# Issuing a kernel's weight stores from ScalarE instead of SyncE, with later steps of an attention and of weight sums moved apart

## The chip, the cores and the metric

The kernel runs on one core of a Trainium2 chip. The metric is the device time of one execution in microseconds. Three executions of the kernel before gave 886.24, 890.32 and 891.84 us, so its median is 890.32 us. One more execution was profiled; it took 885.74 us, of which the program's instructions span 883.8 us.

## The reference

The reference computes a sparse attention and a feed-forward layer behind it, all in float32:

```
scores = scale * q @ k^T                 # 8 batches, 8 heads, 576 positions, 64 per head
heads 0-3: keep keys 0..31 positions back        ("local")
heads 4-7: keep earlier keys of the same position modulo 32   ("strided")
attn = softmax(scores) / (sum + 1e-9);  o = attn @ v
x = o, heads side by side                # 4608 tokens x 512
h = x @ w_in                             # 512 x 2048
g = h where h >= 1, 0 where h <= -1, else (h + 1)^2 / 4
out = g @ w_out                          # 2048 x 512
```

## The kernel before

**Tokens.** The 4608 tokens are done in two ways. The first 1536 go in three chunks of 512, numbered c = 0, 1, 2 (the code calls this number of chunks CLASSIC). The other 3072 go in three blocks of 1024 by a fast matrix product with seven products in place of eight (Winograd's form); those blocks need sums and differences of weight quarters.

**A unit.** In a chunk the 2048 hidden columns go in 16 units f of 128. A unit is twelve TensorE matmuls `up` (line 604), a gate (`bent` on ScalarE, line 608; `squared` on ScalarE, line 611; `gated` on VectorE, line 614), a rounding into a high and a low part (`gh` on ScalarE, line 632; `gl` on VectorE, line 635), and twelve matmuls `down` (line 649), which come two units later. Every product is three matmuls, of high and low parts. The fast blocks use lines 746 and 847 for their matmuls, and lines 696, 699 and 700 for sums and splits of their inputs.

**Preparing the fast blocks.** During chunks 1 and 2 the kernel also writes to DRAM what the fast blocks will load again. `ship` (line 231) stores quarters of unit f's weights, one or two 256 KB transfers per unit, 48 in all (tile `kq`). The sums are made for 16 weight pairs in four steps: `combine` on GpSimd (six instructions, lines 245 and 247), `round_sums` on ScalarE (line 250), a subtraction on VectorE (line 254), and a 1 MB store (line 255, tile `ks`). A pair's sums live in one half of an input tile (`xs`), and there are two halves, so a combine waits for the landing of an earlier store out of its half.

**Order.** The whole order is written out by hand; each engine runs its instructions in the order in which the code names them, and an instruction that waits holds up all that stand behind it on its engine. All transfers are issued by SyncE (SP), in that order too. Time is counted in steps g, four to a unit in chunks 1 and 2 (two after `up`, two after `down`), and in the fast blocks one to six matmuls; a half unit h is two steps. `START` says at which step a batch's attention begins, `LATER` which parts of it come how many steps on, `COMBINE` at which half unit a pair is combined. The function `steps` first emits what TensorE does in a half unit, then the rest.

**A batch's attention.** Batches 2 to 7 run beside the matrix products. Each has four parts u: local 0 and 1, strided 2 and 3. In `LATER`, `s` is scores (line 342), `m x a` mask and subtract the maximum, `e` is the exponential, `q p r` normalise, `t` transposes on VectorE (line 469), `j` stores the result to DRAM (line 479, tile `there`, the spread), `J` loads it back in another layout (line 490, four transfers, tile `pT`, the gather), `v` multiplies by the values (line 505; `V1` does parts 1 and 3, of which part 3 is gathered last), and `h l` copy the products out of PSUM (lines 559 and 568). Scores and products of all batches share two PSUM banks. Loads of the next queries and keys (line 278) and values (line 291) are named right behind the TensorE step that frees their buffer: `fetch_qk` behind `s1` and `s3`, `fetch_v` behind `v0`, `v2` and `V1`.

In the text below, V1(2) is step V1 of batch 2, and h18 is half unit 18, counted from the start of chunk 1; chunk 2 begins at h32. gh(2,15) is gh of chunk 2, unit 15.

Of the kernel before, what the change touches and what calls it, by code (L numbers as in the profile page):

```python
# [8 lines left out]
F32 = mybir.dt.float32  # L9
# [16 lines left out]
def tile_sparse_attention_then_ffn(  # L26
# [14 lines left out]
    nc = tc.nc  # L41
# [107 lines left out]
    def x_tile(s):  # L149
        if s not in xs:  # L150
            xs[s] = slot(f"X{s % 2}", [P, 2, NC, CH], F32, f"xs_{s}")
        return xs[s]

    wt, raws, pieces, held = {}, {}, {}, set()
# [3 lines left out]
    kept = [[(dram.tile([P, 3, 2, HF], F32, tag=f"kq{i}{j}", name=f"kq_{i}_{j}"),  # L158
              dram.tile([P, 4, 2, HF], F32, tag=f"ks{i}{j}", name=f"ks_{i}_{j}")) for j in range(NP)] for i in range(2)]
# [71 lines left out]
    def ship(f, i):  # L231

        j, odd = divmod(f, 2)
        for h in range(2):
            n = (odd, h) if i == 0 else (h, odd)
            if n != (1, 0):
                nc.sync.dma_start(kept[i][j][0][:, sum(n)], wt[f][:, i, h].bitcast(F32))

# [10 lines left out]
    def round_sums(i, j, st):  # L249
        nc.scalar.copy(st[:, :, :HF].bitcast(F32R), st[:, :, HF:])  # L250

    def ship_sums(i, j, st):
        hi, lo = st[:, :, :HF], st[:, :, HF:]
        nc.vector.tensor_tensor(out=lo.bitcast(F32R), in0=lo, in1=hi, op=ALU.subtract)
        nc.sync.dma_start(kept[i][j][1].rearrange("p n x e -> p n (x e)"), st)

    def start_w(*halves):
        for f, i in halves:
            conv_a(f, i)
            conv_b(f, i)  # L260
            conv_c(f, i)
# [354 lines left out]
    def gate(c, f, between=lambda: None):  # L616

        hp = o_ps[c, f]
        u = short(6, F32, f"u_{c}_{f}")
        bent(u, hp)  # L620
        squared(u)
        between()

        if (c, f) == (0, 0):
            o_ps[c, f] = u
        gated(o_ps[c, f], hp, u)
# [64 lines left out]
    def x_sum(m, s, eng=nc.vector):  # L691

        b11, b12, b21, b22 = (x_block(s, r, c) for r in range(2) for c in range(2))
        to, a, b, op = {7: (b12, b22, b12, ALU.subtract), 6: (b11, b12, b11, ALU.add),
                        4: (b21, b21, b11, ALU.subtract), 5: (b12, b22, b11, ALU.subtract)}[m]
        eng.tensor_tensor(out=to, in0=a, in1=b, op=op)
# [5 lines left out]
    def x_split(m, s):  # L702
        xc[m] = slot(X_AT[m], [P, 2, 2, CH], F32R, f"x_{s}_{m}")
        split(xc[m], x_block(s, m in (2, 4, 3), m in (3, 5, 7)))
# [177 lines left out]
    with tc.manual_schedule():  # L882
# [19 lines left out]
        for k in range(2):  # L902
# [10 lines left out]


        START = {2: 0, 3: 39, 4: 74, 5: 119, 6: 156, 7: 240}
        LATER = {0: ("s0", "m0 x0 a0"), 3: ("", "e0"), 6: ("s1", "q0 p0 r0 m1 x1 a1"), 9: ("", "t0 e1"), 11: ("", "j0"),
# [4 lines left out]
        goes = {b: attention(b, lambda u, kind, n: "a") for b in range(1, B)}  # L921

        def steps(g0, g1, which):
            for b, g in START.items():
                for at, names in LATER.items():
                    if g0 <= g + at < g1:
                        goes[b](names[which] if b > 4 else names[which].replace("a", "b").replace("r", "w"))

        def x_steps(s, *todo):
            for m in todo:  # L930
                x_split(m, s) if m > 0 else x_sum(-m, s)
# [1 line left out]


        COMBINE = {h: (n // NP, n % NP, half) for n, (h, half) in enumerate((
            (0, 1), (3, 0), (6, 1), (9, 0), (12, 1), (16, 1), (20, 1), (24, 1),
            (33, 1), (36, 0), (39, 1), (42, 0), (45, 1), (49, 1), (53, 1), (57, 1)))}

        def sums(h):
            for at, do in ((h, combine), (h - 2, round_sums), (h - 3, ship_sums)):  # L940
                if at in COMBINE:
                    i, j, half_ = COMBINE[at]
                    do(i, j, x_tile(at // 32)[:, half_])

        X_FIRST = {9: (1,), 10: (2,), 14: (-7, -6, 7), 15: (-4, -5, 6, 5)}
        pend = []
        for c in range(CLASSIC):
            for f in range(NF):
                g0 = 4 * (NF * (c - 1) + f)
                if c or f > 1:  # L950
                    up(c, f)
                pe, pre, mid, post = ("",) * 4 if c else STEPS.get(f, ("",) * 4)
                go = goes[1]
                go(pe)
                if c:
                    steps(g0, g0 + 2, 0)
                else:
                    start_w(*halves[f])
                go(pre)
                gate(c, f, lambda: go(mid))  # L960
                if c == 0:
                    pend.append((c, f, rounded(c, f)))
                if c == 0:
                    end_w(*halves[f])
                    if f == 9:
                        for i in range(2):
                            load_piece(NF - 2, i)
                        for i, k in ((0, 0), (0, 1), (1, 0)):
                            load_piece(NF - 1, i, k, o_p, "ob", 2)
                    if f == NF - 4:  # L970
                        load_piece(NF - 1, 1, 1, of=2)
                    if f == NF - 3:
                        fetch_qk(2, 0)
                go(post)
                if c:
                    steps(g0, g0 + 2, 1)
                    ship(f, c - 1)
                    sums(g0 // 2)
                    if c == 2:
                        x_steps(0, *X_FIRST.get(f, ()))  # L980
                if c:
                    pend.append((c, f, rounded(c, f)))
                if len(pend) > 2:
                    down(*pend.pop(0))
                if c or f == NF - 1:
                    steps(g0 + 2, g0 + 4, 0)
                    steps(g0 + 2, g0 + 4, 1)
                    sums(g0 // 2 + 1)
        for n in range(3):
            fetch_w(n)  # L990
        for n, a in enumerate(pend):
# [1 line left out]
            for at in range(2):  # L993
                fetch_w(3 + 2 * n + at)
        x_steps(0, 3, 4)
        X_NEXT = {9: (1,), 10: (2,), 11: (-7,), 12: (-6,), 13: (7,), 14: (-4,), 15: (-5,), 16: (6,), 18: (5,), 20: (3,), 27: (4,)}
        for s in range(NSC):
            g0 = 4 * NF * (CLASSIC - 1) + 2 * len(UP) * s

# [6 lines left out]
            def beside_down(n):  # L1006
                for which in range(2):
                    steps(g0 + len(UP) + 2 * n, g0 + len(UP) + 2 * n + 2, which)
                if s + 1 < NSC:
                    x_steps(s + 1, *X_NEXT.get(n, ()))  # L1010

# [61 lines left out]
```

## Time and profile before

| What | Value |
|---|---|
| Median of three runs | 890.32 us |
| The profiled execution | 885.74 us, span 883.8 us |
| TensorE busy | 826.7 us, 94% of the span |
| VectorE busy | 572.4 us, 65% |
| ScalarE busy | 496.3 us, 56% |
| GpSimd busy | 212.2 us, 24% |
| Moved by DMA | 195.09 MB |

In the page and the views, PE is TensorE, PEld its weight load, DVE VectorE, ACT ScalarE, POOL GpSimd, SP SyncE; a q behind the name means its sequencer. Times stand in microseconds from the start of the span. A name such as `xp<-pT` is the written tile and one that is read, and `x12` the number of instructions merged in a row. A wait is put down to what ended it. In a timeline the brackets hold the engine's idle time before the row and what ended it. Chunk 0 ends near 115 us, chunks 1 and 2 fill the time to about 376 us, and the fast blocks the rest.

### The profile page before, as it was taken

The page shows a single profiled execution, that of the slowest core. Times are in us where ns is not written, and L with a number is a line of the kernel's source. Part 1 is how long each engine was busy: PE and PEld are TensorE (multiplying, and loading weights), DVE is VectorE, ACT ScalarE, POOL GpSimd, SP SyncE. Part 2 cuts the span into 40 slices and gives each one's busy share as a digit, 9 for nine tenths or more (in the row PEclk, how much of TensorE's full clock was granted, in tenths as well). Part 3 has the DMA queues.
Part 4 walks back from the last instruction along what each step waited for, and adds up shares of the span by engine and source line. Part 5 has one row for each costly group of instructions (what it writes and reads, how often), then busy time and mean ns, then how long its engine had stood idle before and what let it go on. Part 6 is the DMA issues. An engine that isn't in the chain of part 4 may idle for free.

```text
span 883.8 us, 17886 instructions
## 1 busy us (share of the span) xinstructions
PE 826.7 (94%) x6965; PEld 664.4 (75%) x6965; DVE 572.4 (65%) x846; ACT 496.3 (56%) x876; POOL 212.2 (24%) x220
## 2 busy tenths in 40 slices
PE   8999998797989996799999989999999899999997
PEld 6788876686867775578777867778888678888886
DVE  6898847455647652656666778566577854467564
ACT  6888935343344443466766534558755437676442
POOL 6454352522417234112222000122110000111000
PEclk9999999797999997899999999999999999999999
DMA  9918135857558864588888856787767567666664
GB/s 353 407 62 291 64 109 223 263 208 248 188 198 292 287 223 144 204 254 288 256 267 263 265 168 221 245 245 231 210 190 216 166 220 217 191 193 196 212 199 153
DMA packets 101794, 195.09 MB, mean 221 GB/s; under 512 B 17104, under 2 KB 32464, under 8 KB 99664
## 3 DMA queue, kind: packets, MB, share of 16 engines
q1 hardware_dynamic: 101712, 193.96, 67.6%
q8 instruction: 55, 0.90, 0.4%
q14 instruction: 27, 0.22, 0.1%
HBM read 147.26 MB, written 46.66 MB: 219 GB/s over the span
## 4 chain that ended last, share of the span: by engine, by line
PE 62%; DVE 16%; ACT 10%; DMA 6%; issue 2%; POOL 2%; SPq 2%; ACTq 0%; POOLq 0%; DVEq 0%
PE y L746 13%; PE h L604 10%; PE o L649 9%; PE yo L847 9%; PE z L746 7%; DVE hl L700 5%; PE xo L847 4%; ACT hl L699 3%; PE x L746 3%; PE xp L505 3%; DMA pT<-there 3%; PE sc L342 2%; DMA ks<-xs 2%; SPq L490 1%; DVE gb L802 1%
## 5 line engine op out<-in xcount | busy, mean ns | idle before, releaser
L604 PE MATMUL h<-xq,w 128*128 128x512 f32 x576 | 143.7, 398 | 4.0 <-DVE gl L635 3.1
L746 PE MATMUL y<-x,wr 128*128 128x512 f32 x576 | 141.6, 392 | 0.4 <-ACT ga L754 0.3
L649 PE MATMUL o<-gh,w 128*128 128x512 f32 x384 | 132.8, 407 | 5.7 <-ACT gh L632 4.3
L847 PE MATMUL yo<-hl,wr 128*128 128x512 f32 x576 | 134.4, 391 | 3.4 <-DVE hl L700 3.4
L604 PEld LDWEIGHTS h<-xq,w 128*128 128x128 f32 x576 | 108.8, 191 | 29.7 <-DVE gl L635 4.1
L847 PEld LDWEIGHTS yo<-hl,wr 128*128 128x128 f32 x576 | 107.5, 188 | 28.5 <-DVE hl L700 6.3
L746 PEld LDWEIGHTS y<-x,wr 128*128 128x128 f32 x576 | 107.5, 188 | 24.1 <-ACT ga L754 0.7
L649 PEld LDWEIGHTS o<-gh,w 128*128 128x128 f32 x384 | 74.1, 193 | 23.9 <-ACT gh L632 4.7
L649 PE MATMUL o<-gl,w 128*128 128x512 f32 x192 | 76.8, 400 | 0.7 <-DVE gl L635 0.7
L847 PE MATMUL zo<-hl,wr 128*128 128x512 f32 x288 | 69.1, 394 | 7.1 <-DVE hl L700 4.4
L746 PE MATMUL z<-x,wr 128*128 128x512 f32 x288 | 73.6, 391 | 1.1 <-ACT gab L781 1.1
L245 POOL TENSOR_TENSOR xs<-w 128x512 f32<-128x512 f32 x32 | 42.2, 1337 | 117.5 <-DMA ks<-xs 74.1
L847 PEld LDWEIGHTS zo<-hl,wr 128*128 128x128 f32 x288 | 53.5, 188 | 22.1 <-DVE hl L700 7.0
L614 DVE SCALAR_TENSOR_TENSOR h<-h,u 128x512 f32<-128x512 f32 x47 | 32.7, 695 | 52.7 <-ACT u L611 52.6
L699 ACT CAST hl<-ga 128x1024 fp32r<-128x1024 f32 x36 | 38.1, 1058 | 49.7 <-DVE ga L800 22.1
L700 DVE TENSOR_TENSOR hl<-ga,hl 128x1024 fp32r<-128x1024 f32 x36 | 44.5, 1236 | 33.0 <-ACT hl L699 33.0
L746 PEld LDWEIGHTS z<-x,wr 128*128 128x128 f32 x288 | 53.7, 188 | 12.8 <-ACT gab L781 1.5
L611 ACT ACTIVATE tmp<-tmp 128x512 f32<-128x512 f32 x96 | 60.7, 632 | 3.0
L786 POOL TENSOR_TENSOR ga<-gb,ga 128x1024 f32<-128x1024 f32 x9 | 21.5, 2394 | 165.1 <-DVE ga L614 161.2
L408 POOL TENSOR_TENSOR pr<-pr,st 128x768 f32<-128x768 f32 (+3 forms) x19 | 23.5, 1242 | 134.8 <-DVE st L404 121.1
L608 ACT ACTIVATE u<-h,half 128x512 f32<-128x512 f32 x48 | 32.9, 686 | 40.7 <-PE h L604 40.7
L505 PE MATMUL xp<-pT,v 64*64 64x32 f32 (+2 forms) x1760 | 36.3, 229 | 20.1 <-DMA pT<-there 19.2
(117 smaller groups left out, 1332.1 us busy)
## 6 DMA issues: line engine op xcount, KB each, us to landing
wr<-ks SPq DMA_DIRECT2D x192, 256.0 KB, 3.8
wr<-kq SPq DMA_DIRECT2D x144, 256.0 KB, 3.2
ks<-xs SPq DMA_DIRECT2D x16, 1024.0 KB, 4.6
raw<-in_w SPq DMA_DIRECT2D x30, 512.0 KB, 9.6
kq<-w SPq DMA_DIRECT2D x48, 256.0 KB, 4.8
qk<-in_qk_s SPq DMA_DIRECT2D x16, 604.0 KB, 6.1
qk<-in_qk_l SPq DMA_DIRECT2D x16, 576.0 KB, 5.7
v<-in_v_l SPq DMA_DIRECT2D x21, 384.0 KB, 5.0
```

Of the source, the lines that this page charges most:

```text
L245: nc.gpsimd.tensor_tensor(out=b[:, :, f] if i else b[:, f], in0=hi, in1=lo, op=ALU.add)
L408: eng.tensor_tensor(out=pr, in0=pr, in1=st[:, 0].unsqueeze(2).broadcast_to(list(pr.shape)), op=ALU.add)
L505: nc.tensor.matmul(xp[p][j * D:(j + 1) * D, n], loaded[b, local, b0 + n][keys, j], qs, start=True, stop=True)
L604: nc.tensor.matmul(o_ps[c, f], wt[f][:, 0, h, x, e:e + P], xq[c][:, y, cc], start=first and n == 0, stop=last and n == len(todo) - 1)
L608: nc.scalar.activation(u, h, AF.Relu, bias=half, scale=0.5)
L611: nc.scalar.activation(u, u, AF.Square)
L614: nc.vector.scalar_tensor_tensor(out=to, in0=h, scalar=1.0, in1=u, op0=ALU.max, op1=ALU.min)
L649: nc.tensor.matmul(o_ps[c][d], wt[f][:, 1, h, x, e:e + P], gs[y], start=f == 0 and n == 0, stop=f == NF - 1 and n == 2)
L699: nc.scalar.copy(t[:, 0], src)
L700: nc.vector.tensor_tensor(out=t[:, 1], in0=src, in1=t[:, 0].bitcast(F32), op=ALU.subtract)
L746: nc.tensor.matmul(to, w_[:, a, c * P:(c + 1) * P], xc[m][:, b, c], start=m in (1, 2, 5) and c + q == 0, stop=c == 1 and q == 2, skip_grou ...
L847: nc.tensor.matmul(to, w_[jj][:, a, d * P:(d + 1) * P], t[:, b, jj], start=m in (1, 2, 5) and k + jj + q == 0, stop=k == NP // 2 - 1 and j ...
```

## The change

The change has four parts. `ship` and the store of the sums are issued by ScalarE, not by SyncE. The old `ship_sums` is cut in two: `rest_of_sums` (VectorE) and `ship_sums` (the store), and the steps behind a combine at half unit h move from h+2 (rounding) and h+3 (subtraction and store) to h+3, h+4 and h+5; `COMBINE` itself has new half units. In `LATER`, `v0` stands 6 steps behind its gather where it stood 4, `v2` 7 where it stood 6, `V1` still 5 behind its gather; all from `v0` on stands one or two steps later, and batches 3 to 6 start two, one, four and four steps earlier. The fast block's first input sums (`x_steps`, table `X_FIRST`) are named by half unit: the first two stay where they were, the sums 7 and 6 with split 7 move from h60 to h61, split 5 from h62 to h63. In `X_NEXT`, the same table for the later fast blocks, sum 7 moves one place on.

```diff
     def ship(f, i):
...
-                nc.sync.dma_start(kept[i][j][0][:, sum(n)], wt[f][:, i, h].bitcast(F32))
+                nc.scalar.dma_start(kept[i][j][0][:, sum(n)], wt[f][:, i, h].bitcast(F32))
...
-    def ship_sums(i, j, st):
+    def rest_of_sums(i, j, st):
         hi, lo = st[:, :, :HF], st[:, :, HF:]
         nc.vector.tensor_tensor(out=lo.bitcast(F32R), in0=lo, in1=hi, op=ALU.subtract)
-        nc.sync.dma_start(kept[i][j][1].rearrange("p n x e -> p n (x e)"), st)
+
+    def ship_sums(i, j, st):
+        nc.scalar.dma_start(kept[i][j][1].rearrange("p n x e -> p n (x e)"), st)
...
-        START = {2: 0, 3: 39, 4: 74, 5: 119, 6: 156, 7: 240}
+        START = {2: 0, 3: 37, 4: 73, 5: 115, 6: 152, 7: 240}
...
-                 18: ("v0", "h0 l0"), 20: ("", "J1"), 21: ("s3", "m3 x3 a3 q2 p2 r2"), 24: ("", "t2 e3"), 26: ("", "j2"),
-                 28: ("", "q3 p3 r3"), 29: ("", "J2"), 35: ("v2", "h2 l2 t3"), 37: ("", "j3"), 40: ("", "J3"),
-                 45: ("V1", "h1 l1 h3 l3")}
+                 20: ("v0", "h0 l0"), 21: ("", "J1"), 22: ("s3", "m3 x3 a3 q2 p2 r2"), 25: ("", "t2 e3"), 27: ("", "j2"),
+                 29: ("", "q3 p3 r3"), 30: ("", "J2"), 37: ("v2", "h2 l2 t3"), 39: ("", "j3"), 42: ("", "J3"),
+                 47: ("V1", "h1 l1 h3 l3")}
...
         COMBINE = {h: (n // NP, n % NP, half) for n, (h, half) in enumerate((
-            (0, 1), (3, 0), (6, 1), (9, 0), (12, 1), (16, 1), (20, 1), (24, 1),
-            (33, 1), (36, 0), (39, 1), (42, 0), (45, 1), (49, 1), (53, 1), (57, 1)))}
+            (0, 1), (2, 0), (5, 1), (7, 0), (10, 1), (12, 0), (15, 1), (20, 1),
+            (32, 1), (35, 0), (37, 1), (40, 0), (42, 1), (47, 1), (52, 1), (57, 1)))}
 
         def sums(h):
-            for at, do in ((h, combine), (h - 2, round_sums), (h - 3, ship_sums)):
+            for at, do in ((h - 5, ship_sums), (h - 4, rest_of_sums), (h - 3, round_sums), (h, combine)):
...
-        X_FIRST = {9: (1,), 10: (2,), 14: (-7, -6, 7), 15: (-4, -5, 6, 5)}
+        X_FIRST = {50: (1,), 52: (2,), 61: (-7, -6, 7), 62: (-4, -5, 6), 63: (5,)}
...
-                    if c == 2:
-                        x_steps(0, *X_FIRST.get(f, ()))
+                    x_steps(0, *X_FIRST.get(g0 // 2, ()))
...
+                    x_steps(0, *X_FIRST.get(g0 // 2 + 1, ()))
...
-        X_NEXT = {9: (1,), 10: (2,), 11: (-7,), 12: (-6,), 13: (7,), 14: (-4,), 15: (-5,), 16: (6,), 18: (5,), 20: (3,), 27: (4,)}
+        X_NEXT = {10: (1,), 11: (2,), 12: (-7, -6), 13: (7,), 14: (-4,), 15: (-5,), 16: (6,), 18: (5,), 20: (3,), 27: (4,)}
```

## The prediction

> **What bounds the kernel now.** I first read busy time by stage: chunk 0, chunk 1, chunk 2, the fast blocks (columns: window, length, busy time of PE, PEld, DVE, ACT and POOL with instructions in brackets, granted clock, DMA share, GB/s).
>
> ```profile
> 26.00:115.00 89.00, 88.64 (x823) 71.46 (x822) 78.97 (x150) 77.81 (x155) 40.95 (x41) 1.00 0.52 193
> 115.00:245.00 130.00, 115.67 (x1203) 92.88 (x1202) 74.34 (x130) 50.83 (x97) 53.65 (x58) 0.92 0.63 208
> 245.00:372.00 127.00, 107.59 (x1132) 85.32 (x1131) 72.30 (x108) 54.54 (x109) 47.23 (x47) 0.95 0.67 229
> 372.00:884.00 512.00, 493.47 (x3275) 398.35 (x3273) 328.91 (x416) 296.58 (x468) 55.21 (x39) 1.00 0.71 219
> ```
>
> TensorE is the bound: in chunk 0 and the fast blocks it is busy 99.6% and 96% of the time at clock 1.00. Chunks 1 and 2, where the change is made, are different: 257.0 - 115.67 - 107.59 = 33.7 us idle, and a clock of 0.92 and 0.95. DVE and ACT are busy there only 57% and 41%, less than in chunk 0 (89% and 87%). So waits, not work, cost the time. Next: who TensorE, and the SP queue, waited for in 112 to 372 us (total, times, longest).
>
> ```profile
> PE xp L505 <- DMA pT<-there: 16.7, 6, 6.4
> PE o L649 <- ACT gh L632: 4.3, 1, 4.3
> PE sc L342 <- ACT xs L559: 4.2, 5, 1.7
> PE h L604 <- DVE gl L635: 3.1, 3, 1.4
> SPq L255 <- DVE xs L254: 71.7, 16, 10.0
> ```
>
> Half of TensorE's idle time is attention's value products waiting for their gather. And SP, which issues the gather, stands for 71.7 us before the 16 stores of sums, until VectorE's subtraction is done. That the two belong together is seen in the timeline. Around V1(2), DVE and SP:
>
> ```profile
> 199.94 1.22 DVE L254 TENSOR_TENSOR xs<-xs 128x1024 fp32r<-128x1024 f32 x1
> 189.78 0.89 SPq L479 DMA_DIRECT2D there<-t  x2
> 201.22 0.33 SPq L255 DMA_DIRECT2D ks<-xs  x1
> 201.64 3.01 SPq L490 DMA_DIRECT2D pT<-there  x4
> ```
>
> The spread was issued by 190.67 us. The gather behind it could have followed at its landing, near 194.4 (the page's median landing for these spreads, 3.7 us, is quoted below), but SP stood at the store until 201.2. The chain of waits shows the same order, store and then gather, ahead of the two other large stalls, of v0(2) and V1(4).
>
> **Part 1, the stores leave SP: the three stalls.** What they cost, TensorE's timeline first, then the matmul groups behind each stall from the chain of waits, with one normal group:
>
> ```profile
> 158.63 0.43 PE L505 MATMUL xp<-pT,v 64*64 64x32 f32 x4 [6.27 <-DMA pT<-there]
> 159.56 2.77 PE L505 MATMUL xp<-pT,v 64*64 64x32 f32 x92 [0.50 <-DMA pT<-there]
> 202.47 0.90 PE L505 MATMUL xp<-pT,v 64*64 64x32 f32 x48
> 206.45 0.48 PE L505 MATMUL xp<-pT,v 54*64 54x64 f32 x4 [3.09 <-DMA pT<-there]
> 210.04 1.61 PE L342 MATMUL sc<-qk 64*32 64x64 f32 x48 [1.58 <-DVE xq L568]
> 344.30 0.48 PE L505 MATMUL xp<-pT,v 54*64 54x64 f32 x4 [6.45 <-DMA pT<-there]
> 347.24 2.09 PE L342 MATMUL sc<-qk 64*32 64x64 f32 x96 [0.95 <-ACT xs L559]
> 162.33 4.06 PE h L604 x12
> 211.65 4.94 PE o L649 x12
> 349.33 4.41 PE h L604 x12
> 219.34 2.72 PE o L649 x12
> ```
>
> v0(2): 6.27 + 0.50 waiting; the 92 products take 2.77 where 92 x 0.90/48 = 1.7 is normal (+1.0); the next twelve matmuls 4.06 for 2.72 (+1.34): 9.1 us. V1(2): 3.09, then 1.58 until the PSUM banks are copied out for s1(3), then +2.22: 6.9 us. V1(4): 6.45, 0.95 for the banks, +1.69: 9.1 us. Together 25.1 us.
>
> After the change nothing on SP waits for VectorE's subtraction, and SP loses 64 issues. For v0(2) the product also comes two steps later. I leave 0.5 us of it. V1 keeps its 5 steps; with the spread landed 7 us before SP got to the gather (194.4 to 201.6), a 3.1 us wait would go. But something is late next. In the new order J3(2) and s1(3) share h21, and `steps` names TensorE's part first, so the loads of queries and keys behind s1(3) stand ahead of the gather on SP, and they wait for s1(3) itself. The same pair in the trace (SP), the gather's issue and landing, and the landings of the page:
>
> ```profile
> 166.92 1.16 SPq L278 DMA_DIRECT2D qk<-in_qk_l  x2
> 168.13 2.83 SPq L490 DMA_DIRECT2D pT<-there  x4
> DMA to landing us min/median/max: 2.0/3.6/6.7
> there<-t SPq DMA_DIRECT2D x12, 160.0 KB, 3.7
> ks<-xs SPq DMA_DIRECT2D x16, 1024.0 KB, 4.6
> ```
>
> From the end of s1(3): 1.2 for the loads, about 2.4 to the last gather's issue, 3.6 to 6.7 to land: 7.2 to 10.3 us. TensorE reaches the product that needs it after two groups of 2.72 and 0.90 of V1's first part: 6.3 us. So V1(2) waits 0.9 to 4.0; I take 2, and 1 for the clock: 3 us left. For V1(3) (J3 behind s1(4), h39, but three groups to go) the same sum gives 0 to 1.3; I take 0.
>
> The Trainium skill, "TensorE: Matmul & The Clock Gate", Part 1, says that the clock falls to half only after an idle window of about 3.4 us. By it a 2 us wait has no clock price, and 2 us would be left, not 3; here 3.1 and 1.6 us of waiting, with small matmuls between, were followed by 4.94 us for 2.72.
>
> **Part 2, the new places: PSUM turnarounds.** Where two attention parts of TensorE fall in one half unit, the second waits until ACT and DVE have emptied the banks. At h37 (v2(3), then s0(4)) that cost:
>
> ```profile
> 264.15 0.30 PE L342 MATMUL sc<-qk 64*32 64x64 f32 x2 [1.73 <-ACT xs L559]
> 264.72 1.15 PE L342 MATMUL sc<-qk 64*32 64x64 f32 x94 [0.27 <-ACT xs L559]
> ```
>
> Read off the tables, such pairs were h22, h37, h59; they will be h18 (v2(2), s0(3)), h42 (V1(3), s2(4)), h60 (V1(4), s1(5)), and one in the first fast block (v2(5), s0(6)). h22 and h59 are in the stalls above. So 2.0 goes (h37), 2.0 + 2.0 comes (h18, h42), 1.0 comes (h60, from 0.95): +3.0. Parts 1 and 2: -25.1 + 0.5 + 3 + 3.0 = -18.6 us. In the fast block +2.0 stands against the waits for gathers outside this window, 19.2 (below) - 16.7 = 2.5, which the later products should end: -0.5.
>
> **Part 3, ScalarE gets the issues.** Durations min/median/max in ns, then the sums' other steps:
>
> ```profile
> L237 SPq DMA_DIRECT2D kq<-w x48: 319/444/2564, 115.8 to 361.3; - x48
> L255 SPq DMA_DIRECT2D ks<-xs x16: 319/330/338, 142.2 to 357.1; - x16
> L250 ACT CAST xs<-xs 128x1024 fp32r<-128x1024 f32 x16 | 16.7, 1046 | 19.8 <-POOL xs L247 19.8
> L245 POOL TENSOR_TENSOR xs<-w 128x512 f32<-128x512 f32 x32 | 42.2, 1337 | 117.5 <-DMA ks<-xs 74.1 <-ACT u L611 17.4 <-DVE h L614 10.3
> L247 POOL TENSOR_TENSOR xs<-xs 128x256 f32<-128x256 f32 x64 | 53.2, 831 | 5.0
> L505 PE MATMUL xp<-pT,v 64*64 64x32 f32 (+2 forms) x1760 | 36.3, 229 | 20.1 <-DMA pT<-there 19.2
> ```
>
> 48 x 0.444 + 16 x 0.330 = 26.6 us of ACT's sequencer. ACT's 105.4 us busy in 257 become 132 in about 236, 56%. The `kq` issues wait for nothing (the weights are long there) and stand between the square and gh, where ACT waits for VectorE's gate anyway (0.70 us, line 614). TensorE feels them only where it waits for ACT: the four turnarounds and the two ends of chunks. Bounds 0 and 26.6; six places with about one issue each give 2.5.
>
> The `ks` store now waits on ACT for the subtraction named half a unit earlier. Behind it stand the rounding and gh or the next gate; gl waits for gh, and `down` for both two units later. Bounds: 0, and the 71.7 us that SP stood there. SP came early and ACT does not, so I take a value near 0: 1.5.
>
> The combine now starts at the landing of a store issued in the same half unit: 4.6 + 2 x 1.34 + 4 x 0.83 = 10.6 us to the end of the sums. The rounding comes three half units later, 3 x 236/64 = 11.1 us. Now ACT stands 19.8 us at that rounding, in 6 waits; I take no change, with 5 either way.
>
> **Part 4, the end of chunk 2.** The last `down` waited for gh and gl of (2,15), behind input sums on DVE:
>
> ```profile
> 355.22 0.70 DVE L614 SCALAR_TENSOR_TENSOR h<-h,u 128x512 f32<-128x512 f32 x1 [3.86 <-ACT u L611]
> 368.14 2.41 DVE L700 TENSOR_TENSOR x<-xs,x 128x1024 fp32r<-128x1024 f32 x2
> 370.59 0.69 DVE L635 TENSOR_TENSOR gl<-h,gh 128x512 fp32r<-128x512 f32 x1
> ```
>
> From 355.22 to 371.28 DVE was all but full, 16.1 us. One split (2.41/2 = 1.2) goes behind gl, batch 5's transposes (about 1.0) come in ahead of it: DVE's stretch stays. But V1(4), 88 products or 1.65 us, now lies inside it, so TensorE waits less, and ACT does gh without the split ahead of it. I take -3 of a stall of 4.3 for gh (quoted first) and the slow clock behind it.
>
> **Sum.** -18.6 - 0.5 + 2.5 + 1.5 - 3 = -18.1; from the profiled 885.74 us (883.8 span and 1.9 around it) that is 867.6. The median stands 4.6 above the profiled execution, the lowest run 0.5; I predict 868. This case alone reaches from 857 (nothing of parts 2 and 3 shows, V1(2) does not wait) to 876 (V1(2) waits 4 us, the rounding 5).
>
> **Rivals.** *ScalarE inherits the wait* (slower). If ACT reaches each store as early as SP did, the 71.7 us hold up its rounding and gates. Half of it on TensorE gives 867.6 - 1.5 + 36 = 902. It makes the kernel slower from (18.1 + 1.5)/71.7 = 27% of it on. For: ACT and DVE already wait for each other around line 614. Against: half a unit between subtraction and store. 0.08.
>
> *Only issue time is saved.* Gathers are late because their data stands among 1 MB stores, not because SP stood; on another queue the stores still share the engines. Then V1(2) and V1(4) keep their waits and slow groups, less 2.5 for the bank waits moved elsewhere: +6.9 + 9.1 - 3 - 2.5 = +10.5, 878. For: DMA share is 0.63 to 0.67. Against: SP stood idle 11 us ahead of the gather at 201.64. 0.12. The Trainium skill says it in "DMA: Bandwidth & Descriptors", section "Issuing engines are not separate DMA queues": transfers from all issuers share 16 engines, and another issuer saves only sequencer time; it does not speak of a wait at the head of an issuer's list.
>
> *VectorE is late next.* TensorE's stalls let DVE and ACT catch up; without them, gh and gl (4.3 + 3.1 us now) take half of the gain: 868 + 9 = 877. Against: chunk 0, with DVE at 89% and TensorE full. 0.18.
>
> **Chances.** Forecast 0.62. A difference under 1%, about 9 us, is what a measurement hardly tells from none. Faster by over 1% (under 881.4): the forecast, nearly all of the third rival and most of the second, 0.80; within 1%: their upper ends and a weak first rival, 0.12; slower 0.08. Range 856 to 882: it leaves out the first rival, the second's upper end and the forecast's lowest edge.
>
> **What would show it.** Right: TensorE's waits for gathers in chunks 1 and 2 at 2 to 4 us, not 16.7; the clock there above 0.95; V1(2) the one gather wait left; bank waits at h18, h42, h60; SP never at the stores. Wrong: ACT's stores waiting over 1 us each for line 254, or gh and gl taking the gathers' place.

## The result and the profile after

The kernel after takes 883.15 us (median of 20 executions, 879.41 to 887.41), the kernel before 889.84 us (20 executions). The ratio is 0.9936, with a 95% interval from 0.9918 to 0.9954: 5.7 us faster by the ratio, not 22. The forecast of 868 us was wrong, and its range from 856 to 882 missed the median by 1.2 us. About 4 us of the miss are the base: the forecast took its 18.1 us off the profiled execution (885.74 us), which lies 4.1 us under the median of 889.84. The profiled execution of after took 881.21 us, with a span of 879.1.

How much of that lies in chunks 1 and 2 is read from TensorE's timeline: the first `up` of chunk 1 and the first matmuls of the fast blocks. In before these are:

```profile
117.93 2.88 PE L604 MATMUL h<-xq,w 128*128 128x512 f32 x12
376.19 1.61 PE L746 MATMUL y<-x,wr 128*128 128x512 f32 x6
```

And in after, where the lines behind 255 have moved on by two:

```profile
118.73 2.65 PE L606 MATMUL h<-xq,w 128*128 128x512 f32 x11
370.30 1.52 PE L748 MATMUL y<-x,wr 128*128 128x512 f32 x6
```

The two chunks went from 376.19 - 117.93 = 258.3 us to 251.6. From there to the end of the span it went from 883.8 - 376.19 = 507.6 us to 508.8, and chunk 0 is 0.8 longer. So the whole gain of the profiled execution, 6.7 us, is in chunks 1 and 2; below, "the two chunks" is this length. Busy time of after in the windows of chunks 1 and 2, with the columns shown for before:

```profile
115.00:245.00 130.00, 112.41 (x1187) 88.95 (x1186) 76.96 (x130) 49.28 (x94) 52.31 (x53) 0.93 0.60 211
245.00:372.00 127.00, 116.95 (x1217) 93.60 (x1216) 76.60 (x117) 60.99 (x119) 54.37 (x56) 0.96 0.67 231
```

TensorE still idles 257.0 - 112.41 - 116.95 = 27.6 us where it idled 33.7, and the clock went up by only 0.01 in each chunk. Who TensorE waited for in 112 to 372 us (total, times, longest), and the first row of SP's queue in the same stretch:

```profile
PE h L606 <- DVE gl L637: 8.8, 5, 2.5
PE sc L344 <- DVE xq L570: 6.9, 1, 6.9
PE sc L344 <- ACT xs L561: 3.6, 3, 2.3
PE xp L507 <- DMA pT<-there: 3.3, 3, 1.7
PE xp L507 <- DVE pr L395: 1.7, 1, 1.7
PE o L651 <- DVE gl L637: 0.4, 1, 0.4
SPq L481 <- DVE t L471: 60.3, 12, 8.5
```

The waits for gathers, 16.7 us, are down to 3.3, the 4.3 us for gh at the end of chunk 2 are gone, and SP, which has no more stores of sums, now stands longest for the transposes that a spread carries off (line 471). In their place stand a single wait of 6.9 us for the copies out of PSUM (line 570), and gl at 8.8 where it was 3.1.

ScalarE now issues the stores, and waits at the sums in two places. The first two rows are the issues (count, duration min/median/max in ns, first and last start); the others are from the groups of instructions, with the idle time ahead of a group behind the second bar:

```profile
L237 ACTq DMA_DIRECT2D kq<-w x48: 326/327/1222, 122.4 to 361.7; - x48
L257 ACTq DMA_DIRECT2D ks<-xs x16: 326/326/468, 144.6 to 362.2; - x16
```

```profile
L250 ACT CAST xs<-xs 128x1024 fp32r<-128x1024 f32 x16 | 16.9, 1056 | 33.3 <-POOL xs L247 22.3 <-DMA kq<-w 4.6 <-DMA pT<-there 4.3
L610 ACT ACTIVATE u<-h,half 128x512 f32<-128x512 f32 x33 | 22.7, 687 | 35.5 <-PE h L606 26.4 <-DVE xs L254 8.8 <-ACT st L425 0.2
```

The `bent` of line 610 does not read a sum. Its 8.8 us behind line 254 are the store in front of it on ScalarE, which waits for the subtraction. Some of the 33.3 us ahead of the rounding is of the same kind, though the view names something else. ScalarE's timeline of after, at the worst place:

```profile
279.51 0.63 ACT L613 ACTIVATE u<-u 128x512 f32<-128x512 f32 x1
284.33 0.33 ACTq L257 DMA_DIRECT2D ks<-xs  x1
284.75 1.04 ACT L250 CAST xs<-xs 128x1024 fp32r<-128x1024 f32 x1 [4.61 <-DMA kq<-w]
```

The row blames the landing of a weight store for 4.61 us, but ScalarE stood at the store of sums from 280.14 to 284.33. The gaps ahead of the 16 stores, taken from this timeline in the same way, add up to about 20 us, and eight of them are over 1 us. Of the 33.3 + 8.8 = 42.1 us of the two rows above, then, about 22 are waits for GpSimd at the rounding and 20 are the stores.

The large wait, at h18, is seen best with four engines side by side. Rows of GpSimd, ScalarE, VectorE and TensorE from the timeline of after:

```profile
179.67 2.53 POOL L245 TENSOR_TENSOR xs<-w 128x512 f32<-128x512 f32 x2 [2.56 <-DMA ks<-xs]
182.28 4.41 POOL L247 TENSOR_TENSOR xs<-xs 128x256 f32<-128x256 f32 x4
186.72 1.05 ACT L250 CAST xs<-xs 128x1024 fp32r<-128x1024 f32 x1 [5.05 <-POOL xs L247]
189.66 1.22 DVE L254 TENSOR_TENSOR xs<-xs 128x1024 fp32r<-128x1024 f32 x1
190.91 0.33 ACTq L257 DMA_DIRECT2D ks<-xs  x1
194.97 0.34 ACT L561 COPY xs<-xp 128x108 f32<-128x108 f32 x1 [1.87 <-DMA ks<-xs]
195.35 1.10 DVE L570 TENSOR_TENSOR xq<-xp,xq 128x216 fp32r<-128x216 f32 x2 [1.93 <-ACT xs L561]
195.94 2.16 PE L344 MATMUL sc<-qk 64*32 64x64 f32 x96 [6.93 <-DVE xq L570]
```

Read it upward from the last row. The scores of s0(3) wait for the banks of v2(2) to be copied out. ScalarE's copy writes into the half tile whose sums the store of 190.91 has to carry off first, and that store landed only just before 194.97. The store was late because the rounding, the gate behind it and the subtraction were late, and those because the combine began at 179.67, at the landing of the store before it. So it is one chain through GpSimd, ScalarE, VectorE and a 1 MB transfer, and at its end TensorE waits. The landing itself is the last 1.87 us of it; before that ScalarE was at a gate, a rounding and the store itself, which stand ahead of the copies in its order.

### The profile page after: what moved, and what is told of

It is laid out like the page before. It is cut to its first block, busy times and chain, and to the rows that moved or that the text cites. A ratio compares the mean times of both kernels' runs of the same rounds, so it can differ in the third digit from the quotient of the medians.

```text
span 879.1 us, 17888 instructions
## 1 busy us (share of the span) xinstructions
PE 825.4 (94%) x6965; PEld 662.0 (75%) x6965; DVE 575.3 (65%) x846; ACT 498.6 (57%) x876; POOL 216.0 (25%) x220
## 4 chain that ended last, share of the span: by engine, by line
PE 61%; DVE 18%; ACT 10%; DMA 5%; issue 3%; POOL 1%; SPq 1%; ACTq 0%; DVEq 0%; POOLq 0%
PE y L748 13%; PE h L606 10%; PE o L651 10%; PE yo L849 8%; PE z L748 7%; DVE hl L702 5%; PE xo L849 4%; ACT hl L701 3%; PE x L748 3%; PE xp L507 3%; PE sc L344 2%; DMA pT<-there 2%; DMA ks<-xs 2%; DVE xs L254 1%; DVE xs L698 1%
## 5 line engine op out<-in xcount | busy, mean ns | idle before, releaser
L606 PE MATMUL h<-xq,w 128*128 128x512 f32 x576 | 146.5, 404 | 9.6 <-DVE gl L637 8.8
L245 POOL TENSOR_TENSOR xs<-w 128x512 f32<-128x512 f32 x32 | 44.8, 1421 | 113.5 <-DMA ks<-xs 66.1
L701 ACT CAST hl<-ga 128x1024 fp32r<-128x1024 f32 x36 | 38.0, 1055 | 53.2 <-DVE ga L802 29.4
L247 POOL TENSOR_TENSOR xs<-xs 128x256 f32<-128x256 f32 x64 | 54.6, 853 | 5.0
```

The costliest lines, as they stand in the source:

```text
L245: nc.gpsimd.tensor_tensor(out=b[:, :, f] if i else b[:, f], in0=hi, in1=lo, op=ALU.add)
L247: nc.gpsimd.tensor_tensor(out=st[:, to, HF:], in0=st[:, x, HF:], in1=st[:, y, HF:], op=op)
L606: nc.tensor.matmul(o_ps[c, f], wt[f][:, 0, h, x, e:e + P], xq[c][:, y, cc], start=first and n == 0, stop=last and n == len(todo) - 1)
L701: nc.scalar.copy(t[:, 0], src)
```

## The experiments

The theory ahead of the runs: the gain comes from the gathers, which no longer stand behind a store that waits on SP; part of it is given back by the sums' chain through GpSimd and ScalarE, and by ScalarE's share of the issues. The rivals: the move to ScalarE does the good; the attention steps alone do it; the issues alone eat up the gain. All ratios are against the kernel before, run on the same chip, with their 95% interval. "The two chunks" is the length read above: 258.3 us in before, 251.6 in after.

### Both kinds of stores back on SyncE

```diff
-                nc.scalar.dma_start(kept[i][j][0][:, sum(n)], wt[f][:, i, h].bitcast(F32))
+                nc.sync.dma_start(kept[i][j][0][:, sum(n)], wt[f][:, i, h].bitcast(F32))
...
-        nc.scalar.dma_start(kept[i][j][1].rearrange("p n x e -> p n (x e)"), st)
+        nc.sync.dma_start(kept[i][j][1].rearrange("p n x e -> p n (x e)"), st)
```

> All of the change but its first part: both kinds of store are issued by SyncE again, every step stands where the changed kernel has it. My theory now (A): what the forecast missed is that ScalarE stands at the 1 MB stores for VectorE's subtraction, about 26 us in all, and that its gates come late for it. By A the gl waits of TensorE in chunks 1 and 2 fall from 8.8 to about 4 us and the time is 4 to 6 us under the changed kernel's (877 to 879). Rival B, the forecast's own reason: SyncE stands at the stores again, gathers are late again (over 10 us of waits in place of 3.3), and the time is 888 or more. Rival C, the new steps alone made the small gain and nothing hangs on the issuer: 883, within 2 us of the changed kernel.

Measured: 878.17 us, 0.9870 (0.9840 to 0.9899); the two chunks 246.5 us. TensorE's, SP's and ScalarE's waits of this kernel in 112 to 372 us:

```profile
PE sc L344 <- DVE xq L570: 8.2, 2, 7.7
PE h L606 <- DVE gl L637: 7.7, 5, 2.8
SPq L257 <- DVE xs L254: 39.3, 13, 8.0
ACT xs L250 <- POOL xs L247: 32.4, 10, 5.6
```

And the wait at h18, from TensorE's timeline:

```profile
194.64 2.16 PE L344 MATMUL sc<-qk 64*32 64x64 f32 x96 [7.66 <-DVE xq L570]
```

TensorE does not wait for a gather at all, although SP still stands 39.3 us at the stores. The move to ScalarE did not bring the gain; here it costs (0.9936 - 0.9870) x 889.8 = 5.9 us, and the two intervals don't meet. The time is the one that theory A expected, but not for its reason: gl fell from 8.8 only to 7.7 us, not to 4, and the larger part of what left the waits is the 3.3 us for gathers that after still had. The wait at h18 is as long as in after, so it doesn't come from ScalarE issuing the store.

### Only the 48 weight blocks back on SyncE

```diff
-                nc.scalar.dma_start(kept[i][j][0][:, sum(n)], wt[f][:, i, h].bitcast(F32))
+                nc.sync.dma_start(kept[i][j][0][:, sum(n)], wt[f][:, i, h].bitcast(F32))
```

> The changed kernel with the 48 stores of 256 KB on SyncE again; the 1 MB stores stay on ScalarE. Issue time alone: 48 x 0.33 = 16 us leave ScalarE. If issue time is what hurts (rival E), 878 to 880; by theory A, by which the waits at the 1 MB stores hurt, 882 to 884, since these 48 wait for nothing.

Measured: 881.27 us, 0.9902 (0.9879 to 0.9926). It lies halfway between after and the first run, in neither of the two expected ranges: by the ratios 3.0 us for the 48 small issues, 2.8 us for the 16 large ones that wait for the subtraction. But the intervals overlap those of both neighbours, and in the profiled execution the two chunks take 251.8 us, as in after (251.6). So this run doesn't show how the 5.9 us divide.

### After, with 48 more issues on ScalarE

```diff
                 nc.scalar.dma_start(kept[i][j][0][:, sum(n)], wt[f][:, i, h].bitcast(F32))
+                more = dram.tile([16, 128], F32, tag=f"more{f}{i}{h}", name=f"more_{f}_{i}_{h}")
+                nc.scalar.dma_start(more, wt[f][:16, i, h, 0, :128].bitcast(F32))
```

> The changed kernel with 48 more stores of 8 KB issued by ScalarE, one behind each store of 256 KB, into a place that nothing reads. It prices an issue on ScalarE: moving the 48 stores off ScalarE gained 3.0 us (0.9936 to 0.9902). If issues are what costs (rival E), these cost 2 to 4 us more, 885 to 887; if the 3 us had another cause (the bytes, the queue), 883 within 1.5.

Measured: 889.40 us, 1.0002 (0.9981 to 1.0022). Its issues, from the view of that line:

```profile
L239 ACTq DMA_DIRECT2D more<-w x48: 324/446/1887, 122.5 to 371.0; - x48
```

48 issues of 8 KB, which wait for nothing, cost (1.0002 - 0.9936) x 889.8 = 5.9 us, 0.12 us each: about a quarter of the 0.446 us that one takes, and more than the 2 to 4 us expected. So 48 more issues, on this engine, can eat all that the change won. Their transfers of 8 KB were not priced apart from the issues.

### The attention steps alone

Before, with the new `START` and `LATER` and nothing else.

```diff
-        START = {2: 0, 3: 39, 4: 74, 5: 119, 6: 156, 7: 240}
+        START = {2: 0, 3: 37, 4: 73, 5: 115, 6: 152, 7: 240}
...
-                 18: ("v0", "h0 l0"), 20: ("", "J1"), 21: ("s3", "m3 x3 a3 q2 p2 r2"), 24: ("", "t2 e3"), 26: ("", "j2"),
+                 20: ("v0", "h0 l0"), 21: ("", "J1"), 22: ("s3", "m3 x3 a3 q2 p2 r2"), 25: ("", "t2 e3"), 27: ("", "j2"),
...
```

> The kernel before with only START and LATER of the changed one: attention's steps moved, stores and sums as before. Rival C: 883 to 885, the gain comes from here. By the forecast's reasons about 880 to 884, since v0(2) no longer waits (9 us) but V1(2) and V1(4) still stand behind SyncE's wait, and two more turnarounds come. Rival D, the new places cost: 888 to 892.

Measured: 886.72 us, 0.9963 (0.9937 to 0.9989); the two chunks 256.8 us. Waits in 112 to 372 us, with before's line numbers:

```profile
SPq L255 <- DVE xs L254: 64.7, 15, 8.4
PE sc L342 <- ACT xs L559: 11.5, 4, 5.8
PE xp L505 <- DMA pT<-there: 7.0, 6, 1.7
```

Products further behind their gather take 9.7 of the 16.7 us, and the bank waits of line 559 rise from 4.2 to 11.5, three quarters of that. With SP at the stores for 64.7 us, six waits for gathers are left. The time lies between what the forecast's reasons and rival C give (880 to 885) and what rival D gives (888 to 892): the moved steps help and cost at once.

### The sums' steps alone

Before's `START` and `LATER`, both stores on SyncE, with the new spacing of the sums and the new input tables; in `COMBINE` the first three half-0 entries stand one half unit earlier (its diff is below, with the run of half 0). The diff is against after; the lines of `LATER` are left out.

```diff
-                nc.scalar.dma_start(kept[i][j][0][:, sum(n)], wt[f][:, i, h].bitcast(F32))
+                nc.sync.dma_start(kept[i][j][0][:, sum(n)], wt[f][:, i, h].bitcast(F32))
...
-        nc.scalar.dma_start(kept[i][j][1].rearrange("p n x e -> p n (x e)"), st)
+        nc.sync.dma_start(kept[i][j][1].rearrange("p n x e -> p n (x e)"), st)
...
-        START = {2: 0, 3: 37, 4: 73, 5: 115, 6: 152, 7: 240}
+        START = {2: 0, 3: 39, 4: 74, 5: 119, 6: 156, 7: 240}
...
```

> The kernel before with only the sums' later steps moved apart (rounding at h+3, subtraction h+4, store h+5, all stores on SyncE, new combines, half tile 0 one half unit earlier, new places of the input sums); attention's steps as before. If the half unit between subtraction and store is what frees SyncE for the gathers, the three large gather waits shrink from 16.7 to under 6 us without any help of ScalarE's queue, and the time is 877 to 882. By the forecast's reasons, that the stores must leave SyncE, 885 to 890.

Measured: 883.69 us, 0.9942 (0.9919 to 0.9964). Waits in the same stretch:

```profile
SPq L257 <- DVE xs L254: 32.4, 10, 8.5
PE sc L344 <- ACT xs L561: 8.1, 5, 4.2
PE h L606 <- DVE gl L637: 7.6, 4, 3.8
PE o L651 <- DVE gl L637: 4.6, 1, 4.6
```

No wait for a gather is left, with the products as close behind their gathers as before and the stores on SP. So the new steps of the sums end them, with no help of ScalarE's queue: SP still stands at ten of the 16 stores, but 32.4 us in all where it stood 71.7. Whether it is the half unit between subtraction and store or the new places of the combines, no run tells apart; both were changed here. The time missed both ranges, since what comes up instead is gl, at chunk 2's end too, and the banks.

### The sums' steps and ScalarE's issues, without the new attention steps

The kernel of the run before this one, but with both stores on ScalarE: after with before's `START` and `LATER`, and half 0 earlier.

```diff
-                nc.sync.dma_start(kept[i][j][0][:, sum(n)], wt[f][:, i, h].bitcast(F32))
+                nc.scalar.dma_start(kept[i][j][0][:, sum(n)], wt[f][:, i, h].bitcast(F32))
...
-        nc.sync.dma_start(kept[i][j][1].rearrange("p n x e -> p n (x e)"), st)
+        nc.scalar.dma_start(kept[i][j][1].rearrange("p n x e -> p n (x e)"), st)
```

> The changed kernel with START and LATER of the kernel before (attention's steps back where they were), and the combines of the second half tile one half unit earlier so that the last of them is stored before attention writes there. Theory A: the late gates stay (gl waits 8 us or more), the time is within 3 us of the changed kernel's. Rival D, the new places of attention's parts cost what was gained: the 6.9 us wait at h18 and the 2.3 us one at h42 go, the old turnarounds of 1.6, 1.7 and 1.0 us return, v0(2) may wait 1 to 3 us for its gather; 876 to 879.

Measured: 884.59 us, 0.9931 (0.9905 to 0.9958), against 0.9942 with the stores on SyncE. Here the issuer makes no difference that can be measured, and rival D's 876 to 879 is ruled out; theory A's signs, gl at 8 us or more (it is 8.5) and a time within 3 us of after's, came true, but the issuer is not what they show, since the time is the same without it. So the 5.9 us are not a fixed price of 64 issues; they are a price in the order with the new attention steps. One thing differs in the traces: the gaps ahead of the 16 stores, counted in ScalarE's timeline as above, are about 4.5 us here and 20 in after. Whether that is why ScalarE's time is cheap in the old order was not settled.

### Half 0 combined one half unit earlier

From the first run (stores on SyncE):

```diff
-            (0, 1), (2, 0), (5, 1), (7, 0), (10, 1), (12, 0), (15, 1), (20, 1),
+            (0, 1), (1, 0), (5, 1), (6, 0), (10, 1), (11, 0), (15, 1), (20, 1),
```

> The changed kernel with all stores on SyncE (878.17 us, ratio 0.987) and the first half of the combines into half tile 0 one half unit earlier, at 1, 6 and 11, so that the last store out of it is named at h16 and not at h17, one half unit ahead of attention's writes into the same place at h18. Theory F: the 7.7 us wait at h18 is the copies of v2(2) waiting for that store's landing and for ScalarE, which comes late from the rounding; then the wait falls to 2 to 4 us and the time by 3 to 5, to 873 to 875. Theory G: the wait is only two attention parts in one half unit; then nothing changes, 877 to 879.

Measured: 874.67 us, 0.9845 (0.9817 to 0.9873); the two chunks 245.6 us. TensorE in its timeline, and its waits in 112 to 372 us:

```profile
167.43 2.00 PE L344 MATMUL sc<-qk 64*64 64x54 f32 x40 [4.71 <-DVE xq L570]
194.53 0.30 PE L344 MATMUL sc<-qk 64*32 64x64 f32 x2 [2.75 <-DVE xq L570]
```

```profile
PE sc L344 <- DVE xq L570: 7.7, 3, 4.7
PE h L606 <- DVE gl L637: 5.2, 4, 2.5
PE sc L344 <- ACT xs L561: 4.0, 3, 2.7
```

The wait at h18 goes from 7.7 us (first run) to 2.75, as theory F expected, but another of 4.71 us opens at 167 us. Together they are 7.46 us, and the scores of s0(3) start at 194.53 us, in the first run at 194.64. So the edit splits the wait and doesn't shorten it: the copy ahead of s0(3) still waits for a landing of sums (ScalarE's line 561, at 193.57 us, 193.68 in the first run), and TensorE only gets there later. That the time fell into F's range, 873 to 875, was luck as far as h18 goes: the two chunks are 0.9 us shorter, and the ratio is lower than the first run's 0.9870 only with overlapping intervals. The same edit with the stores left on ScalarE:

> The changed kernel, stores on ScalarE as there, with half tile 0 one half unit earlier. By F the 6.9 us wait at h18 shrinks here too and the time falls by 2 to 4, to 879 to 881; against the same order with the stores on SyncE (874.67) it prices the move to ScalarE a second time, 5 us by theory A and E, 0 by C.

Measured: 880.47 us, 0.9896 (0.9873 to 0.9919). Against after it is 0.4% lower, the intervals just touching; against the run with SyncE it is (0.9896 - 0.9845) x 889.8 = 4.5 us slower, again with intervals that just touch: the second measurement of the issuer's price. The wait at h18 is split here too and not shorter in all, 6.14 us at 167 and 3.06 us at 194, so the expected time came out without the expected reason.

### Batch 3 two steps later, so that s0(3) doesn't meet v2(2)

From the first run, and from the one with half 0 earlier:

```diff
-        START = {2: 0, 3: 37, 4: 73, 5: 115, 6: 152, 7: 240}
+        START = {2: 0, 3: 39, 4: 73, 5: 115, 6: 152, 7: 240}
```

> The changed kernel with all stores on SyncE, and batch 3 starting at step 39, as in the kernel before, not 37: s0(3) comes at h19, a half unit behind v2(2), and J3(2) no longer shares h21 with s1(3). By G the h18 wait (7.7 us) is gone, and so is the turnaround at h42: 868 to 872. By F part of it remains, since ScalarE is late anyway and the copies wait for the store: TensorE then waits 2 to 5 us for s0(3) or for gl a little later, 873 to 876.

> Stores on SyncE, half tile 0 one half unit earlier, and batch 3 at step 39. By F and G together the h18 wait is gone and nothing waits for the store there: 870 to 873. By H it gains nothing over 874.67, since ScalarE and VectorE come late for whatever is next (as with step 39 alone, which gave 876.76 where 878.17 was to be beaten): 873 to 876.

Measured: 876.76 us, 0.9878 (0.9844 to 0.9911), against 0.9870 without it; and 873.95 us, 0.9815 (0.9801 to 0.9830), against 0.9845. The bank wait moves. In the first of the two, line 344's wait for line 570 falls from 8.2 to 4.0 us (s0(3), now a half unit behind v2(2), still waits 3.76 us and starts at 195.42), but the products then wait 6.9 us for VectorE to read scores out of the banks (line 395); in the second it is 3.2 and 6.4 us. So theory G, that the two parts in one half unit are the whole wait, is not borne out by the first. The first time is a little above both ranges; the second lies in the one that theory H gives. The second is the fastest version of the study with all sums made, not separated from the one with half 0 earlier alone.

### Batch 5 two steps later

From the run with half 0 earlier: batch 5's products at the end of chunk 2 come two steps later.

```diff
-        START = {2: 0, 3: 37, 4: 73, 5: 115, 6: 152, 7: 240}
+        START = {2: 0, 3: 37, 4: 73, 5: 117, 6: 152, 7: 240}
```

> Stores on SyncE, half tile 0 one half unit earlier, and batch 5 at step 117, so that s1(5) no longer shares h60 with V1(4) (a 1.1 us bank wait and a slow group behind it). G: 871 to 873. H: 873 to 876.

Measured: 885.57 us, 0.9942 (0.9926 to 0.9958), against 0.9845: 8.6 us slower. Two of its waits:

```profile
PE o L651 <- ACT gh L634: 4.3, 1, 4.3
PE o L651 <- DVE gl L637: 2.6, 1, 2.6
```

The stall of before at the end of chunk 2 is back, where neither theory had expected more than 876. What ended it in after was the earlier start of batch 5; the run with the attention steps alone has only 0.5 us of it left, too.

### A shorter combine

From the run with half 0 earlier, with only the first two of GpSimd's six instructions for each combine. Four are left out, so the sums are not the wanted ones.

```diff
-        for to, x, y, op in ((3, 2, 3, ALU.add), (2, 0, 2, ALU.subtract), (0, 3, 0, ALU.subtract), (1, 1, 0, ALU.subtract)):
-            nc.gpsimd.tensor_tensor(out=st[:, to, HF:], in0=st[:, x, HF:], in1=st[:, y, HF:], op=op)
```

> As the run with half tile 0 one half unit earlier (874.67 us, ratio 0.9845), but each combine is its first two GpSimd instructions of six; the four of line 247 (3.3 us a combine) are left out, so the sums that are stored are not the wanted ones. It asks what is next: if it is ScalarE standing at the rounding for GpSimd (29.4 us in 9 waits), theory H, those waits fall under 8 us, the turnarounds shrink with them, and the time falls by 4 to 8, to 867 to 871. If the two-banks order of the attention parts alone is what is left (G), 873 to 875.

Measured: 867.20 us, 0.9720 (0.9695 to 0.9745); the two chunks 235.2 us instead of 245.6. ScalarE's wait at the rounding in the run with half 0 earlier, then TensorE's and ScalarE's waits in this one in 112 to 372 us, with the line numbers two lower:

```profile
ACT xs L250 <- POOL xs L247: 29.4, 9, 5.3
PE sc L342 <- DVE xq L568: 4.3, 2, 4.0
PE h L604 <- DVE gl L635: 3.7, 3, 1.6
PE sc L342 <- ACT xs L559: 2.6, 4, 1.1
ACT xs L248 <- POOL xs L245: 15.4, 7, 3.3
```

Nothing but some 53 us of GpSimd's work is gone (the row of line 247 in before), on an engine that is busy less than half of these chunks, and the kernel is 11.1 us faster. ScalarE stands 15.4 us at the rounding, not 29.4 (under 8 had been expected). All three kinds of TensorE's waits shrink, 7.7 + 5.2 + 4.0 = 16.9 us to 10.6, and the granted clock of chunks 1 and 2 rises from 0.95 and 0.96 to 0.97 and 0.97. The scores of s0(3) start at 189.39 us, 5 us earlier. It is not that the other engines work faster beside an idler GpSimd: VectorE's subtraction takes 1329 ns on average where it took 1337, and ScalarE's rounding 1054 ns in both. So the length of the combine, felt through the chain of the sums, sets a good part of what is left.

## Why the prediction was wrong, point by point

**How far off.** The terms for chunks 1 and 2 were -18.6 + 2.5 + 1.5 - 3 = -17.6 us; the two chunks came out 6.7 us shorter. Of the 10.9 us between, most is found again in two kinds of waits: 4.9 us more than forecast at h18 (part 2) and 5.7 us more for gl in front of `up` (part 3). The terms put at too little are the copies at h18 and the chain of the sums behind the combine; both rest on the same omission, that the sums now set when other work can start.

**Part 1, the gathers: the sum was near, the reason wrong.** Waits for gathers fell from 16.7 to 3.3 us; I had left 0.5 us for v0(2), 3 for V1(2), clock included, and nothing for V1(3). The trace of after has none for v0(2), 0.72 us for V1(3), and for V1(2) 1.66 + 0.96 us and twelve matmuls of 4.59 us behind them where 3.03 is normal, 4.2 us in all. But the step "after the change nothing on SP waits for VectorE's subtraction" is not what did it. With the stores on SP and the sums' steps spread, no gather is waited for (first run, sums' steps alone); with the products moved and SP at the stores for 64.7 us, 7.0 us are left. The sums' new steps were enough, with the stores on SyncE.

**Part 2, the banks: the places were right, one price was not.** Waits stand at h18, h42 and h60 as forecast, at 6.93, 2.31 and 1.13 us against 2.0, 2.0 and 1.0. At h18 I priced the copies out of the banks by the row of h37 and did not ask which tile the copy writes: it is the half tile of the sums, which must have been stored first. In before, two of ScalarE's copies (line 559) already waited 7.4 us for such a landing, so the question could have been asked. The scores behind it were slow as well, 2.16 us where 1.17 is normal. The 5 us too little here are one of the two large errors.

**Part 3, the issues: forecast 4.0 us in all, measured 5.9 and 4.5 us** with the new attention steps, and nothing that can be measured with the old. The split was 2.5 + 1.5; no run shows the split. For the large stores, the issue itself and the wait for the subtraction were not separated. My sign for "wrong", waits of more than 1 us ahead of the stores, came in half of the 16.

**Part 3, the rounding: "I take no change" is the other step that failed.** ScalarE stood 19.8 us at the rounding before. In after it stands 42.1 us there or at the stores ahead of it, of which 22.3 are put down to GpSimd; with the stores on SP, where ScalarE stands at no store, the wait for GpSimd alone is 32.4 us. The sum of 10.6 us against 11.1 was too fine to lean on: GpSimd's combine at 179.67 took 2.53 + 4.41 us where I had put 2 x 1.34 + 4 x 0.83 = 6.0, and a combine that starts late passes its delay on to ScalarE, VectorE, the store and the next combine. gl went from 3.1 to 8.8 us, and the new part is three waits of 2.0 to 2.5 us. One of them, at 327.63, hangs on ScalarE, which came late out of the rounding:

```profile
323.72 1.05 ACT L250 CAST xs<-xs 128x1024 fp32r<-128x1024 f32 x1 [4.80 <-POOL xs L247]
```

The other two, at 155.95 and 177.91, hang on VectorE itself: its timeline has no gap in the 4 us ahead of gl, and the subtraction of the sums, in its new place among attention's work, takes 2.30 and 1.76 us. This is the third rival (VectorE's gl takes the gathers' place), with the sums as its cause through two engines; that a shorter combine brings gl from 5.2 to 3.7 us agrees. I had given it 0.18 and 9 us.

**Part 4, the end of chunk 2: -3 was too little.** Of 4.3 us for gh and 0.7 for gl, 0.4 is left. Batch 5 two steps later brings 6.9 us of waiting back, so the earlier start of batch 5, which I had counted only as one more load on VectorE, is what did it.

**The fast blocks:** -0.5 was forecast; the rest of the span is 1.2 us longer in the profiled executions. In the table `X_NEXT` the entries 1 and 2 move one place on as well, not sum 7 alone; what that does was not tried.

**The sum in the waits.** Off TensorE's waits in 112 to 372 us went 13.4 (gathers) and 4.6 us (end of chunk 2). On came 5.7 (gl in front of `up`), 4.7 (banks: 6.9 + 3.6 against 4.2 + 1.6) and 1.7 us (line 395, which had none). That leaves -5.9 us, against -6.1 of idle time and -6.7 us for the two chunks. So next to nothing was won on slow matmuls, which made up about 6 of the 25.1 us of the three stalls: the clock I wanted above 0.95 came to 0.93 and 0.96, and new waits have slow matmuls of their own.

**The rivals.** ScalarE inherited some of SP's wait, about 20 us of the 71.7. I had it turn the sign once TensorE feels 27% of the 71.7; the whole price of the issuer, 4.5 to 5.9 us, is 6 to 8% of it. "Only issue time is saved" gave a time nearer to the measured one, 878, but by the wrong mechanism: V1(4), which it keeps late, doesn't wait at all. The Trainium skill, "DMA: Bandwidth & Descriptors", section "Issuing engines are not separate DMA queues", counts only the sequencer's time in favour of another issuer. The traces agree that hardly any bandwidth came with it (208 and 229 GB/s in chunks 1 and 2 of before, 211 and 231 in after). The runs show another side: on an engine that computes, that time can be paid, here 4.5 and 5.9 us in two orders and nothing that can be measured in a third.

## What to carry to other kernels

When a queue stands at an instruction that waits, first try to move the instruction further behind what it waits for; handing it to another engine moves the wait to a place where, as here, it may cost more. Before pricing a wait that is taken away, follow what every engine writes next and whose transfer has to leave that tile first. And an engine that is half idle can still set the time, if its work is one link of a chain through engines that wait in order.

## What the runs showed of the hardware

**Issues on a computing engine.** A DMA issue takes 0.33 to 0.45 us of ScalarE's sequencer at the median, and the size doesn't tell (0.327 us for 256 KB, 0.326 for 1 MB, 0.446 for 8 KB above). 48 that wait for nothing cost 5.9 us of the kernel in the order of after.

**Short waits and the clock.** Three waits of TensorE for gl in after, from the timeline, one from the run with batch 3 two steps later, and the granted clock in the windows of the twelve matmuls behind the first two (the column behind the busy times):

```profile
155.95 3.04 PE L606 MATMUL h<-xq,w 128*128 128x512 f32 x12 [2.21 <-DVE gl L637]
177.91 4.59 PE L606 MATMUL h<-xq,w 128*128 128x512 f32 x12 [2.49 <-DVE gl L637]
327.63 4.61 PE L606 MATMUL h<-xq,w 128*128 128x512 f32 x12 [2.00 <-DVE gl L637]
184.84 3.02 PE L606 MATMUL h<-xq,w 128*128 128x512 f32 x12 [3.63 <-DVE gl L637]
```

```profile
155.95:159.00 3.05, 3.05 (x18) 2.26 (x20) 1.19 (x3) 1.76 (x3) 2.36 (x4) 1.00 0.92 361
177.90:182.50 4.60, 4.59 (x13) 3.66 (x14) 2.83 (x4) 2.19 (x5) 2.75 (x3) 0.63 0.72 254
```

After 2.21 us of waiting the clock stayed at 1.00; after 2.49 us it was 0.63, and the wait cost 1.6 us more than its length. It is not the length alone that decides: after 2.00 us the clock was 0.63 too, and after 3.63 us it stayed at 1.00. What else decides, these traces don't show. The Trainium skill, "TensorE: Matmul & The Clock Gate", Part 1, has the clock fall after an idle window of about 3.4 us; a single idle stretch of 2.00 us was enough here, so the measurement decides against taking waits under that length as free of a clock price. For a forecast, a wait of 2 to 3 us may cost its length or 1.6 us more.

**GpSimd's additions are not of one length.** The same two additions of line 245 took 2.53 us at 179.67 and 3.49 us at 188.50, by GpSimd's timeline (whose spans are rough), and the four of line 247 behind them 4.41 and 3.14 us. A sum that fits by half a microsecond, as mine did, has no margin against that.
